# Denominators in four quarters of TensorE's columns, and eight weight operations ahead of the FFN's loop

## The chip, the cores and the metric

The kernel runs on one core of a Trainium2 chip. The time is the device time of one execution in microseconds; the comparison is between medians of several runs.

## The reference

Three stages run one after the other. `B, H, S, D` are 4, 8, 1152, 64; neighbouring queries are averaged in pairs, which leaves 576 queries per head and 2304 tokens of width 512.

```python
q_pool = q.reshape(B, H, S // 2, 2, D).mean(axis=3)
scores = matmul(q_pool, k.transpose(0, 1, 3, 2)) / sqrt(D)
attn = exp(scores - max(scores, -1))
x = matmul(attn / (sum(attn, -1) + 1e-9), v)     # then [2304, 512]
h = x @ w_in                                     # 512 -> 2048
x = (h / (1 + exp(-1.702 * h))) @ w_out          # 2048 -> 512
do_compute = x @ w_skip > 0
logits = x @ w_gate                              # 8 experts
e = argmax(logits); gate = softmax(logits)[e]
out = x; out[do_compute] += gate * (relu(x @ w1[e]) @ w2[e])
```

The weights `w_in` and `w_out` arrive as 64-bit floats.

## The kernel before, in words

Most products on TensorE are of split numbers: an operand is a high part in a reduced fp32 format plus a low part with what is left, and a product is the sum of three.

**Attention** (`attention`, L127) works on 16 pairs of heads; a pair's two heads lie in partitions 0 to 63 and 64 to 127. The loop at the end of the function counts steps, 14 (`NU`) per pair. A step runs one score unit (`score_unit`, L263: products on TensorE, then one exponential on ScalarE into `E`), one unit of row maxima for a pair 19 steps ahead (`max_unit`, L216: products, then a maximum on VectorE), at some steps a group of value products (`av_group`, L300), and sums of `E` on GpSimd (`sum_unit`, L276), whose result is `ds`. At step 10 of pair p stands `den(p - 1)` (L320), which sums `ds` over the 128 partitions by a product with ones: four fp32 products of 288 columns, for each head and half of its queries, into the tile `dn`; ScalarE copies `dn` to `dr`; and one row per head goes to `DEN` in DRAM, by SP's queue (by ScalarE's queue for the last pair). Right behind it in the same step runs `max_rows_put` (L241) for the next pair: a transpose of the row maxima on TensorE (tile `mt`), a high and a low part on VectorE (`mh`, `ml`), and eight DMAs that lay them out in two rows of `M2` (printed as `M` in the profile). The first score unit of the next pair subtracts the maxima by a product of `M2` with ones as the last of its accumulations. Each queue works in the order in which the code issues.

`recip` (L404) reads a batch's denominators back, takes reciprocals on VectorE, and writes them to `RD`.

**The FFN** (`ffn`, L491) takes the tokens in six chunks (`CH`, L34) of 768, 384, 256, 256, 256 and 384; a chunk of 768 is worked in two pieces of 384, the one of 384 in one. For each chunk it goes over 16 blocks (`fb`) of 128 hidden units. A step of the main loop (from L757) is one block and one piece: `layer1` (L591) makes `h` by 12 products on TensorE, a sigmoid on ScalarE, `g = h * sigmoid` on VectorE (L605), the high part `gh` on ScalarE (L606), and the low part `gl` on VectorE (L609). `layer2` follows two steps later (`LAG`) with nine products into `acc`. `h` has two buffers, so the products of step s+2 wait for `g` of step s.

In chunk 0 (32 steps) the weights are converted from 64-bit floats as they are first used. The weights of a block come as two units, `w_in` and `w_out`; a unit takes seven operations on VectorE (L453 to L459) and three on ScalarE (L461 to L463): `wload` (L423) loads it, `wsplit` (L432) gives the operations, and the generator `blocks` (L528) puts them in order. `fill(k)` (L565) gives out the next k of them; `layer1` calls it twice, for 3 and 3 operations in the first piece of a block, 3 and 4 in the second. A unit's first ScalarE operation, the absolute value (L461), is given out when its turn begins, with the load of the unit two ahead; the other two wait in a list that `act` (L571) empties right behind `gh`. Two blocks (`EARLY`) are converted in attention already.

For chunk 1, `xload` (L466) loads X and the reciprocals `RD`, each row of `RD` spread over 64 partitions, into `xraw`, which has one buffer; `xnorm` (L474) multiplies them on VectorE, and `xsplit` (L585) makes the high and low part. The four such loads and products are set down in an agenda, which runs what is due at the end of a step.

**The experts** (`experts`, L874) follow when the last chunk is routed.

Of the kernel before, what the change touches and what calls it, by code (L numbers as in the profile page):

```python
# [9 lines left out]
F32 = mybir.dt.float32  # L10
# [5 lines left out]
AF = mybir.ActivationFunctionType  # L16
# [3 lines left out]
P = 128  # L20

B, H, S, D = 4, 8, 1152, 64
Q = S // 2
HQ = Q // 2
# [15 lines left out]
def pieces(n):  # L40
    k = -(-n // 384)
    return [(i * (n // k), n // k) for i in range(k)]
# [29 lines left out]
class Kernel:  # L72
# [54 lines left out]
    def attention(self, ctx):  # L127
        nc = self.nc
        V, G = nc.vector, nc.gpsimd
        dma = self.dma  # L130
        sm = self.pool(ctx, "a_sm", 2)
# [3 lines left out]
        const = self.pool(ctx, "a_const")  # L135
# [7 lines left out]
        HALF = [slice(64 * u, 64 * u + 64) for u in range(2)]  # L143
        M2 = [const.tile([P, Q], F32R, name=f"M2_{i}") for i in range(2)]
        BD = [const.tile([P, P], F32R, name=f"BD{i}") for i in range(2)]
        ONE = const.tile([P, P], F32R, name="ONE")
        one = const.tile([P, 64], F32, name="one")
        warm = const.tile([P, 2], F32, name="warm")
        V.memset(warm, 0.0)
        nc.scalar.activation(warm[:, 1:2], warm[:, 0:1], AF.Copy)  # L150
# [12 lines left out]
        ag = Agenda()  # L163
# [155 lines left out]

        def den(p):  # L320
            ds = st[p]["ds"]
            dr = sm.tile([P, Q], F32, name="dr", tag="dr", bufs=1)
            ps = slot.tile([P, 2, 512], F32, name="dn", tag="sl")
            for c in range(2):
                for u in range(2):
                    nc.tensor.matmul(ps[HALF[u], c, :HQ], one, ds[:, u, c * HQ:c * HQ + HQ], start=True, stop=True)
            nc.scalar.activation(dr.rearrange("p (a b) -> p a b", a=2), ps[:, :, :HQ], AF.Copy)
            b, hp = divmod(p, H // 2)
            eng = nc.scalar if p == N - 1 else nc.sync
            for u in range(2):  # L330
                eng.dma_start(self.DEN[hp * 2 + u:hp * 2 + u + 1, b * Q:b * Q + Q], dr[64 * u:64 * u + 1])

        LEAD = 19

# [7 lines left out]
        start = {1: [(k_low, 0)], 2: [(q_low, 0)], 4: [(loads, 2)], 5: [(q_add, 1)], 7: [(q_high, 1)], 8: [(k_high, 1, 0)], 9: [(k_high, 1, 1)],  # L342
                 10: [(k_high, 1, 2)], 11: [(v_load, 0)], 13: [(q_add, 2)]}
# [28 lines left out]
        for g in range(-LEAD, NU * N + 20):  # L372
            p, i = divmod(g, NU)
# [117 lines left out]
    def ffn(self, ctx):  # L491
        nc = self.nc
# [6 lines left out]
        sm = self.pool(ctx, "m_sm", reuse_waits="tile")  # L499
        const = self.pool(ctx, "m_const", reuse_waits="tile")  # L500
        hp = self.pool(ctx, "m_h", 2, space=PSUM, reuse_waits="tile")
# [12 lines left out]
        def constants():  # L514
            nc.gpsimd.memset(ONE, 1.0)
            nc.gpsimd.memset(U, 1.0)
            nc.gpsimd.affine_select(out=U, in_=U, compare_op=ALU.is_ge, fill=0.0, base=-1, pattern=[[1, P]], channel_multiplier=-1)
            nc.gpsimd.iota(idi, pattern=[[P, NT]], base=0, channel_multiplier=1)
            for t, step, base in ((w8, -1, 8), (b8, NTOK, 0)):
                nc.gpsimd.iota(i8, pattern=[[step, 8]], base=base, channel_multiplier=0)  # L520
                for i in range(3):
                    nc.gpsimd.tensor_copy(t[:, i], i8)
            V.memset(mac[0], 0.0)

        fq = []
        ag = Agenda()
# [38 lines left out]
        def fill(k):  # L565
            for _ in range(k):
                f = fq.pop(0) if fq else next(splits, None)
                if f:
                    f()

        def act():  # L571
            while after:
                after.pop(0)()
# [17 lines left out]
        def layer1(c, fb, pc, fa, fb_):  # L591
            n = pieces(CH[c])[pc][1]
            h = hp.tile([P, 512], F32, name="h", tag="h")[:, :n]
            ah, al = self.W[fb, "wih"], self.W[fb, "wil"]
            k = 0
            for d in range(ND):
                xh, xl = self.xtile(c, d, pc)
                for a, x in ((ah, xh), (ah, xl), (al, xh)):
                    nc.tensor.matmul(h, a[:, d * P:d * P + P], x, start=(k == 0), stop=(k == 3 * ND - 1))  # L599
                    k += 1  # L600
            g = gp.tile([P, 384], F32, name="g", tag="g")[:, :n]
            gh = g3.tile([P, 384], F32R, name="gh", tag="gh")[:, :n]
            gl = g3.tile([P, 384], F32R, name="gl", tag="gl")[:, :n]
            nc.scalar.activation(g, h, AF.Sigmoid, scale=1.702)  # L604
            V.tensor_tensor(g, h, g, op=ALU.mult)  # L605
            nc.scalar.activation(gh, g, AF.Copy)  # L606
            act()
            fill(fa)
            V.tensor_tensor(gl, g, gh, op=ALU.subtract)  # L609
            fill(fb_)  # L610
            G[c, fb, pc] = (gh, gl)
# [139 lines left out]
                fq.append(fin)  # L751

        constants()
        steps = [(c, fb, pc) for c in range(len(CH)) for fb in range(NF) for pc in range(len(pieces(CH[c])))]
        first = {(c, fb): g for g, (c, fb, pc) in reversed(list(enumerate(steps)))}
        LAG = 2
        for g in range(len(steps) + LAG):  # L757
            ag.now = g
            if g < len(steps):
                c, fb, pc = steps[g]  # L760
                fa, fb_ = (2, 3) if CH[c] >= 384 else (1, 2)
                if g == 2:
                    self.recip(sm, B - 1, ag, 3)
                if c == 0:
                    fa, fb_ = 3, 3 + pc
                layer1(c, fb, pc, fa, fb_)
                if fb == 0 and pc == 0 and c + 1 < len(CH):
                    for j in range(ND):
                        for q in range(len(pieces(CH[c + 1]))):
                            g0 = first[0, 12] + 2 * j - 1 if c == 0 else first[c, 4] + 2 * j  # L770
                            ag.at(g0, xload, c + 1, j, q)
                            ag.at(g0 + 1, xnorm, c + 1, j, q)
                            ag.at(first[c, NF - 1] if c == 0 else g0 + 4, xsplit, c + 1, j, q)
            if g >= LAG:
                c2, f2, p2 = steps[g - LAG]
                layer2(c2, f2, p2)
                if f2 == NF - 1:
                    if c2 == 0 and p2 == 0:
                        while splits.gi_frame:
                            fill(1)  # L780
                            act()
                        rctx.close()
                        late["o"] = self.pool(ctx, "m_o", 2)
                        late["wg"] = late["o"].tile([P, 9, DM], F32, name="wg", tag="wg", bufs=1)
                        dma(late["wg"][:, 0:8], self.wgT.partition_broadcast(P))
                        dma(late["wg"][:, 8], self.w_skip.partition_broadcast(P))
                        for d in range(ND):
                            dma(wgd[:, d, 0:8], self.wgT[:, d * P:d * P + P].rearrange("e p -> p e"))
                            dma(wgd[:, d, 8:9], self.w_skip[d * P:d * P + P].rearrange("(p a) -> p a", a=1))
                    o, n = pieces(CH[c2])[p2]  # L790
                    grp = tuple((C0[c2] + o) // P + i for i in range(n // P))
                    if c2 < len(CH) - 1:
                        todo.extend((grp, i) for i in range(len(grp)))
            if g < len(steps) + LAG - 1:
                rstep()
                ag.run(g)
            if not (self.first or todo or fq or live[0]) and self.listed == NT - CH[-1] // P:

                self.first = late["o"].tile([P, 9, DM], F32, name="first", tag="wg", bufs=1)
                for m in range(4):  # L800
                    self.first_expert_load(m)
                for m in range(8):
                    ag.at(max(g + 2 + m // 2, first[len(CH) - 1, m] + LAG + 1), self.first_expert_split, m)

                ps = hp.tile([P, 8], F32, name="cn", tag="h")
                nc.tensor.matmul(ps, ONE, mac[self.listed], start=True, stop=True)
                V.tensor_scalar(self.early, ps[:, 0:1], P - 0.5, float(P), op0=ALU.is_gt, op1=ALU.mult)
                dma(self.ids_e, self.LIST[0:P])
                V.memset(self.x_e, 0.0)
                nc.gpsimd.indirect_dma_start(  # L810
                    out=self.x_e, out_offset=None, in_=self.X2[0:C0[-1]],
                    in_offset=bass.IndirectOffsetOnAxis(ap=self.ids_e[:, 0:1].bitcast(U32), axis=0),
                    bounds_check=C0[-1] - 1, oob_is_err=False,
                )
# [270 lines left out]
```

## Time and profile before

| what | us |
|---|---|
| median of 3 runs | 1052.24 |
| the runs | 1047.6 to 1054.67 |
| the profiled execution, its time | 1049.92 |
| its span, first to last instruction | 1048.1 |
| TensorE busy in it | 996.8 |
| VectorE busy in it | 768.9 |
| ScalarE busy in it | 501.9 |
| GpSimd busy in it | 454.2 |

All rows of the trace are from the one profiled execution; its times count from the first instruction. Attention ends near 442.7 us, chunk 0 of the FFN takes from there to about 585 us. In the profile PE is TensorE's products and PEld its weight loads, DVE is VectorE, ACT ScalarE, POOL GpSimd, SP the queue of DMAs. "x2" at the end of a row of a timeline tells how many like instructions are merged in it; what stands in brackets is how long the engine was idle before, and what ended that. The end of a product is modelled, so products are read by their starts.

### The profile page before, as it was taken

Reading aid. Unit: us, or ns where it says so; the run is one execution under the profiler, and the core shown is the slowest. Engines: PE = TensorE matmul, PEld = TensorE weight load, DVE = VectorE, ACT = ScalarE, POOL = GpSimd, SP = SyncE. Lnnn points to the kernel's source line nnn. Section 1 sums busy time; section 2 is a strip of 40 time slices with the busy share of each in tenths; the row PEclk is TensorE's granted clock in tenths of the full one; section 3 lists DMA queues with packets and bytes.
Section 4 is the critical chain, followed back from the end, with each engine's and each line's share of the span. In section 5 each row is a group of like instructions: output and inputs, shape, how many; then the busy total and the mean of one; then the engine's idle time right before and its main releaser. Section 6 shows DMA issues by size and latency. Waiting matters only on the chain. (4 is left out here: it accounts for less than half of the span.)

```text
span 1048.1 us, 18986 instructions
## 1 busy us (share of the span) xinstructions
PE 996.8 (95%) x7002; PEld 787.3 (75%) x7002; DVE 768.9 (73%) x1643; ACT 501.9 (48%) x928; POOL 454.2 (43%) x306
## 2 busy tenths in 40 slices
PE   6999999999999999999997999999999997998994
PEld 4766667666766676698886888888889885876773
DVE  7767777778877778799977689787575564656824
ACT  2555555555555554655644422332333261555723
POOL 3798999999999998500000001101111003223212
PEclk9999999999999999999999999999999998998998
DMA  4232232223333322333342520212211234738501
GB/s 166 67 101 81 81 101 82 81 81 97 97 96 96 97 72 71 99 102 122 123 132 81 173 71 16 71 33 60 71 48 44 81 115 145 266 105 285 164 21 51
DMA packets 64321, 103.34 MB, mean 99 GB/s; under 512 B 18630, under 2 KB 34630, under 8 KB 64072
## 3 DMA queue, kind: packets, MB, share of 16 engines
q1 hardware_dynamic: 60068, 96.34, 28.6%
q0 software_dynamic: 3904, 5.15, 1.6%
q8 instruction: 67, 1.10, 0.4%
q14 instruction: 54, 0.44, 0.1%
q10 hardware_dynamic: 228, 0.30, 0.1%
HBM read 90.04 MB, written 17.35 MB: 102 GB/s over the span
## 5 line engine op out<-in xcount | busy, mean ns | idle before, releaser
L233 DVE TENSOR_REDUCE mx<-xs 128x1 f32<-128x384 f32 x432 | 212.7, 550 | 75.5 <-PE xs L230 70.1
L274 ACT ACTIVATE E<-ss 128x640 f32<-128x640 f32 (+1 forms) x224 | 174.0, 787 | 149.0 <-PE ss L273 120.7
L290 POOL TENSOR_TENSOR acc<-acc,E 128x640 f32<-128x640 f32 (+1 forms) x94 | 179.4, 1909 | 16.4 <-ACT E L274 12.3
L310 PE MATMUL av<-E,v 128*64 128x256 f32 (+1 forms) x1152 | 157.1, 413 | 0.0
L599 PE MATMUL h<-xh,wih 128*128 128x384 f32 (+1 forms) x448 | 141.3, 315 | 9.9 <-ACT wih L463 7.7
L599 PE MATMUL h<-xh,wil 128*128 128x384 f32 (+1 forms) x448 | 140.0, 312 | 0.6 <-DVE wil L459 0.5
L599 PE MATMUL h<-xl,wih 128*128 128x384 f32 (+1 forms) x448 | 139.9, 312 | 0.1
L476 POOL TENSOR_TENSOR xa<-xraw 128x256 f32<-128x256 f32 (+1 forms) x16 | 15.5, 970 | 261.3 <-DMA xraw<-RD 256.1
L310 PEld LDWEIGHTS av<-E,v 128*64 128x64 f32 x1152 | 75.6, 136 | 56.0 <-issue 15.0
L626 PE MATMUL acc<-woh,gl 128*128 128x512 f32 x288 | 114.8, 399 | 0.0
L624 PE MATMUL acc<-woh,gh 128*128 128x512 f32 x288 | 114.8, 399 | 0.0
L625 PE MATMUL acc<-wol,gh 128*128 128x512 f32 x288 | 114.5, 398 | 0.0
L230 PE MATMUL xs<-kh,qh 64*128 64x384 f32 x384 | 101.9, 388 | 7.9 <-ACT kh L210 7.2
L273 PE MATMUL ss<-qh,kh 64*128 64x320 f32 (+1 forms) x576 | 107.3, 339 | 2.0 <-ACT E L274 2.0
L604 ACT ACTIVATE g<-h 128x384 f32<-128x384 f32 (+1 forms) x112 | 49.4, 441 | 116.1 <-PE h L599 116.0
L606 ACT ACTIVATE gh<-g 128x384 fp32r<-128x384 f32 (+1 forms) x112 | 53.8, 480 | 104.6 <-DVE g L605 104.6
L599 PEld LDWEIGHTS h<-xh,wih 128*128 128x128 f32 x448 | 84.2, 188 | 18.5 <-ACT wih L463 11.0
L643 DVE CUSTOM_DVE_ANT_0 junk<-xs,wg 128x512 bf16<-128x512 f32 x135 | 95.5, 707 | 2.0
L605 DVE TENSOR_TENSOR g<-h,g 128x384 f32<-128x384 f32 (+1 forms) x112 | 55.7, 497 | 55.9 <-ACT g L604 54.5
L273 PE MATMUL ss<-M,ONE 64*128 64x320 f32 (+1 forms) x576 | 94.2, 294 | 0.7 <-DMA M<-ml 0.6
L273 PE MATMUL ss<-qh,kl 64*128 64x320 f32 (+1 forms) x576 | 92.2, 293 | 0.0
L273 PE MATMUL ss<-ql,kh 64*128 64x320 f32 (+1 forms) x576 | 92.1, 293 | 0.0
(195 smaller groups left out, 2069.6 us busy)
## 6 DMA issues: line engine op xcount, KB each, us to landing
stage<-w SPq DMA_DIRECT2D x40, 512.0 KB
qd<-qT SPq DMA_DIRECT2D x16, 576.0 KB
v<-v SPq DMA_DIRECT2D x16, 576.0 KB
kr<-kT SPq DMA_DIRECT2D x15, 576.0 KB
wr<-w_in SPq DMA_DIRECT2D x16, 512.0 KB
wr<-w_out SPq DMA_DIRECT2D x16, 512.0 KB
X<-xs SPq DMA_DIRECT2D x18, 256.0 KB
out<-xs SPq DMA_DIRECT2D x18, 256.0 KB
```

Source lines behind the costliest of these rows:

```text
L230: nc.tensor.matmul(ps[:, :384], q, k[:, part * 384:part * 384 + 384], start=True, stop=True)
L233: V.reduce_max(o, ps[:, :384], axis=AX.X)
L273: nc.tensor.matmul(ps[:, u, j * w:j * w + w], k[HALF[u]], q[HALF[u], qs], start=(n == 0), stop=(n == 3))
L274: nc.scalar.activation(place(p, i), ps[:, :, :len(kbs) * w], AF.Exp, scale=0.5 / D ** 0.5)
L290: G.tensor_tensor(d["a"], d["a"], place(p, i), op=ALU.add)
L310: nc.tensor.matmul(d["av"][HALF[u], :w], d["v"][:, u, kb], e[:, u, n * w:n * w + w], start=(kb == 0), stop=(kb == KB - 1))
L599: nc.tensor.matmul(h, a[:, d * P:d * P + P], x, start=(k == 0), stop=(k == 3 * ND - 1))
L605: V.tensor_tensor(g, h, g, op=ALU.mult)
L624: nc.tensor.matmul(acc[t], gh[:, ts], bh, start=(fb == 0), stop=False)
L625: nc.tensor.matmul(acc[t], gh[:, ts], bl, start=False, stop=False)
L626: nc.tensor.matmul(acc[t], gl[:, ts], bh, start=False, stop=(fb == NF - 1))
L643: V.tensor_tensor_reduce(out=junk, in0=R[grp[i]], in1=late["wg"][:, e], op0=ALU.mult, op1=ALU.add, scale=1.0, scalar=0.0, accum_out=R[grp] ...
```

## The change

There are two parts. In `den` the tile of ones gets 32 columns instead of 64, and the four products write four quarters of the partitions of one bank; the copy then has 288 columns instead of 576, and four rows of 288 go to `DEN` instead of two of 576. In `ffn`, `fill(8)` stands ahead of the main loop, so the first eight operations of the conversion stand ahead of step 0's; and the loads for chunk 1 are due two steps sooner (steps 21, 23, 25, 27 instead of 23 to 29), each product one step sooner and two steps behind its load instead of one.

```diff
-        one = const.tile([P, 64], F32, name="one")
+        one = const.tile([P, 32], F32, name="one")
...
         def den(p):
             ds = st[p]["ds"]
-            dr = sm.tile([P, Q], F32, name="dr", tag="dr", bufs=1)
+            dr = sm.tile([P, HQ], F32, name="dr", tag="dr", bufs=1)
             ps = slot.tile([P, 2, 512], F32, name="dn", tag="sl")
-            for c in range(2):
-                for u in range(2):
-                    nc.tensor.matmul(ps[HALF[u], c, :HQ], one, ds[:, u, c * HQ:c * HQ + HQ], start=True, stop=True)
-            nc.scalar.activation(dr.rearrange("p (a b) -> p a b", a=2), ps[:, :, :HQ], AF.Copy)
+            quarter = [(slice(64 * u + 32 * c, 64 * u + 32 * c + 32), u, c) for u in range(2) for c in range(2)]
+            for to, u, c in quarter:
+                nc.tensor.matmul(ps[to, 0, :HQ], one, ds[:, u, c * HQ:c * HQ + HQ], start=True, stop=True)
+            nc.scalar.activation(dr, ps[:, 0, :HQ], AF.Copy)
             b, hp = divmod(p, H // 2)
             eng = nc.scalar if p == N - 1 else nc.sync
-            for u in range(2):
-                eng.dma_start(self.DEN[hp * 2 + u:hp * 2 + u + 1, b * Q:b * Q + Q], dr[64 * u:64 * u + 1])
+            for to, u, c in quarter:
+                eng.dma_start(self.DEN[hp * 2 + u:hp * 2 + u + 1, b * Q + c * HQ:b * Q + c * HQ + HQ], dr[to.start:to.start + 1])
...
         constants()
+        fill(8)
         steps = [(c, fb, pc) for c in range(len(CH)) for fb in range(NF) for pc in range(len(pieces(CH[c])))]
...
-                            g0 = first[0, 12] + 2 * j - 1 if c == 0 else first[c, 4] + 2 * j
+                            g0 = first[0, 12] + 2 * j - 3 if c == 0 else first[c, 4] + 2 * j
                             ag.at(g0, xload, c + 1, j, q)
-                            ag.at(g0 + 1, xnorm, c + 1, j, q)
+                            ag.at(g0 + 2 if c == 0 else g0 + 1, xnorm, c + 1, j, q)
```

## Rows read from the trace of the kernel before

**Rows 1.** The page's first part: busy time of each engine, share, instructions.

```profile
PE 996.8 (95%) x7002; PEld 787.3 (75%) x7002; DVE 768.9 (73%) x1643; ACT 501.9 (48%) x928; POOL 454.2 (43%) x306
```

**Rows 2.** Busy time by stretch: its length, PE, PEld, DVE, ACT, POOL, clock, DMA, GB/s.

```profile
92.00:118.00 26.00, 26.00 (x256) 18.16 (x254) 20.18 (x35) 14.49 (x23) 23.81 (x14) 1.00 0.28 82
...
450.00:460.00 10.00, 10.00 (x51) 8.94 (x50) 10.00 (x24) 6.50 (x13) 0.00 (x0) 1.00 0.43 134
...
550.00:560.00 10.00, 7.04 (x28) 6.38 (x29) 8.11 (x17) 4.75 (x9) 0.00 (x0) 0.83 0.29 96
```

**Rows 3.** TensorE's timeline around one pair's denominators: start, length, line, tiles, count.

```profile
94.92 1.14 PE L326 MATMUL dn<-ds,one 128*64 128x288 f32 x8
...
95.41 0.66 PE L326 MATMUL dn<-ds,one 128*64 128x288 f32 x4
...
95.65 0.41 PE L326 MATMUL dn<-ds,one 128*64 128x288 f32 x2
95.99 0.28 PE L243 MATMUL mt<-ident,m 128*9 128x128 f32 x1
96.20 0.39 PE L273 MATMUL ss<-qh,kh 64*128 64x256 f32 x2
```

**Rows 4.** Groups on ScalarE in attention, by shape: busy us, mean ns, idle before.

```profile
L327 ACT ACTIVATE dr<-dn 128x576 f32<-128x576 f32 x15 | 9.8, 654 | 8.0 <-PE dn L326 8.0
...
L314 ACT ACTIVATE ev<-av 128x320 f32<-128x320 f32 x15 | 6.6, 437 | 13.6 <-PE av L310 13.6
```

**Rows 5.** The timeline of SP's queue behind the same denominators.

```profile
96.79 0.53 SPq L331 DMA_DIRECT2D DEN<-dr  x2
97.41 2.47 SPq L252 DMA_DIRECT2D M<-mh  x4
100.01 2.40 SPq L252 DMA_DIRECT2D M<-ml  x4
```

**Rows 6.** The timeline of weight loads at the next pair's first score unit.

```profile
102.72 0.20 PEld L273 LDWEIGHTS ss<-ql,kh 64*128 64x128 f32 x2
102.87 0.29 PEld L273 LDWEIGHTS ss<-M,ONE 64*128 64x128 f32 x2
```

**Rows 7.** TensorE's timeline: first products of steps 0, 2, 26, 28, 32, 33.

```profile
442.67 0.44 PE L599 MATMUL h<-xh,wih 128*128 128x384 f32 x1
...
446.93 0.34 PE L599 MATMUL h<-xh,wih 128*128 128x384 f32 x1
...
552.96 0.45 PE L599 MATMUL h<-xh,wih 128*128 128x384 f32 x1 [3.72 <-ACT wih L463]
...
566.05 0.44 PE L599 MATMUL h<-xh,wih 128*128 128x384 f32 x1 [2.90 <-ACT wih L463]
...
584.99 0.34 PE L599 MATMUL h<-xh,wih 128*128 128x384 f32 x1
...
589.18 0.34 PE L599 MATMUL h<-xh,wih 128*128 128x384 f32 x1
```

**Rows 8.** VectorE's timeline: the start of the FFN, and the first two products for chunk 1.

```profile
441.93 0.06 DVE L523 MEMSET mac<- 128x4 uint32 x1
445.57 0.56 DVE L605 TENSOR_TENSOR g<-h,g 128x384 f32<-128x384 f32 x1 [3.58 <-ACT g L604]
...
550.28 0.56 DVE L476 TENSOR_TENSOR xa<-xraw 128x384 f32<-128x384 f32 x1 [2.34 <-DMA xraw<-RD]
...
563.38 0.56 DVE L476 TENSOR_TENSOR xa<-xraw 128x384 f32<-128x384 f32 x1 [2.82 <-DMA xraw<-RD]
```

**Rows 9.** ScalarE's timeline at the start of the FFN.

```profile
442.79 0.65 ACT L327 ACTIVATE dr<-dn 128x576 f32<-128x576 f32 x1 [0.99 <-PE dn L326]
443.47 0.55 ACTq L331 DMA_DIRECT2D DEN<-dr  x2
...
446.60 1.21 ACT L461 ACTIVATE t<-wr 128x512 f32<-128x512 f32 x2
```

**Rows 10.** The timeline of SP's queue: the first two loads of `RD`.

```profile
543.10 0.53 SPq L83 DMA_DIRECT2D xraw<-RD  x1
...
555.23 0.52 SPq L83 DMA_DIRECT2D xraw<-RD  x1
```

## The prediction

> **What bounds the kernel now.** I read the engines' busy times first, then busy time by stretch, then the timelines of single engines around the two places that the diff touches. Over the whole span TensorE is busy 996.8 of 1048.1 us [rows 1], so a saving counts if TensorE gets to its next work sooner. The stretches say where that is open. In attention, 92 to 118 us, TensorE is busy 26.00 of 26.00 us [rows 2]: attention costs what TensorE's queue costs, unless something else makes it wait. In the FFN's first chunk it is different. A step is 4.19 us when nothing waits (584.99 to 589.18), the first two, without second-layer products, together 4.26 us (442.67 to 446.93) [rows 7]. Step 32, the first of chunk 1, would so start at 442.67 + 4.26 + 30 x 4.19 = 572.6 us. It starts at 584.99 [rows 7]: 12.4 us are stalls. From 550 to 560 us TensorE is busy 7.04 of 10 us and its mean granted clock is 0.83 of 2.4 GHz, a mean between the levels 2.4 and 1.2, behind a wait of 3.72 us for a converted `wih` [rows 2, 7]. From 450 to 460 VectorE is the full one, 10.00 of 10 us for 24 instructions, 0.42 us each [rows 2].
>
> Why the weights come late: a pair of steps gives VectorE 6 + 7 = 13 weight operations, and a block needs 14. Two blocks are ready at the start, so the conversions slide one operation per block from just early to just late. The last step of the slide is made worse by two waits of VectorE for `xraw` (2.34 and 2.82 us, ended by the broadcast of `RD`) [rows 8]: behind them stand `g`, the rest of the weight operations, and TensorE's waits of 3.72 and 2.90 us [rows 7].
>
> **Edit 1, the denominators on TensorE.** Now a pair's denominators are 8 passes (four products of two passes each), two side by side: four waves, 0.24 us apart (95.41 to 95.65), the first at 94.92 [rows 3]. After the last wave `mt` starts 0.34 us later, 0.10 more than a wave; from `mt` to the scores it is 0.21 us, for 128 columns, where a wave of 288 takes 0.24, so 0.11 for the product and again 0.10 for the change of tile shape [rows 3]. Four side by side make two waves: 2 x 0.24 = 0.48 us less. Between the value products (64 columns) and the denominators (now 32) a change of shape appears, 0.10 us. TensorE saves 0.38 us per pair. No row shows four abreast: the ends are no gain (four waves, minus 0.10) and 0.48 us (the change after them falls away); I take two waves, since two abreast start in one row.
>
> **Edit 1, the copy and the DMAs.** ScalarE's copy of 576 columns takes 0.65 us; the nearest row to 288 is 320 columns, 0.44 us [rows 4], so about 0.40: 0.25 saved. But the two DMAs to `DEN` become four on SP's queue, and behind them in that queue stand the eight that build the next pair's row maxima `M`. Two cost 96.79 to 97.41, 0.31 us each with what lies between; eight for `M` follow at 0.6 us each until 102.41 [rows 5]. TensorE's first score unit of the next pair needs `M`: its two weight loads lie at 102.87 and take 0.29 us together, where the pair before took 0.20 [rows 6]. The second was held 0.1 us by the semaphore, without delaying a product: `M` lands just as TensorE arrives, slack at most some 0.05 us. So this chain, not TensorE's queue, decides what edit 1 is worth. Last wave of the denominators: earlier by 2 x 0.24 - 0.10 = 0.38. Copy: 0.25 earlier. DMAs: 2 x 0.31 = 0.62 later. Sum: 0.01 us earlier. TensorE gains 0.38 us on the denominators and waits about 0.3 of it for `M`. With the slack I take 0.06 us per pair, times 14 pairs that have both: 0.8 us. If the queue were no limit: 14 x 0.38 = 5.3 us.
>
> The Trainium skill bears on the four abreast. "TensorE: Matmul & The Clock Gate", section "Part 3: Packing small matmuls — row/col tiling", says that products in different column groups run at once, and gives 2.38 times the rate for three. No run here shows that yet. By that efficiency, an estimate from the page, four would take some 0.6 us instead of 0.48, and the sum would lose 14 x 0.12 = 1.7 us.
>
> The last pair's copy and DMAs are on ScalarE: 0.25 less, two more issues of 0.27 us (0.55 for two) [rows 9]; nothing at TensorE's end of it, since its later products wait for VectorE's last sums as before.
>
> **Edit 2a, eight weight operations first.** VectorE is free from 441.99 to 445.57 [rows 8]. The eight are in order a first one, then seven; the second needs ScalarE's absolute value. That comes behind the copy and four issues: 442.79 + 0.40 + 4 x 0.27 = 444.3, and 0.6 for itself (1.21 for two) [rows 9]: 444.9. Seven operations at 0.42 end at 447.85, and only then comes `g` of step 0, 0.56 us: 448.4 instead of 446.13. Step 2 needs that buffer of `h` and started at 446.93 [rows 7]: TensorE stalls 1.5 to 1.7 us, I take 1.6. Step 2's second-layer products need `gl` only after another 2.5 us, by when three fills and `gl` fit. From there VectorE spends about 3.9 us per step (6.5 fills and two `g` operations at 0.42 plus) against TensorE's 4.19, so nothing more is lost; the weights stand eight operations earlier, a bit over half a block, more than the slide of one per block eats up to the last block. `wih` then is converted one whole step before its use in blocks 10 to 15, and these waits go.
>
> **Edit 2b, the next chunk's operands.** The loads of X and RD come two steps earlier, each product one step earlier and two steps (8.4 us) behind its load. RD was issued at 543.10 and 555.23, VectorE went on at 550.28 and 563.38: 7.2 and 8.15 us [rows 8, 10]. One step could not cover that, two do, nearly: with the load's issue and the product itself the cycle is 8.2 to 9.2 us. VectorE may come up to 0.8 us late per load. But its lateness has cover now: `g` of step s is needed only at step s+2, and the weights are a step ahead. I allow 0.3 us. On SP's queue these loads pass two or three weight loads, each held until VectorE frees its buffer; the first may so wait for one `g` and one weight operation more, about 1 us.
>
> Sum: of 12.4 us stalls 1.6 + 0.3 remain, 10.5 gained, and 0.8 in attention: 11.3 us. All later stages follow chunk 0 and shift with it. The profiled execution took 1049.92 us, so 1038.6 beside it; it lies 2.3 us under the median of the three runs, 1052.24, from which I forecast 1040.9 us.
>
> **Rivals.** (A) `M` has more slack than I read, and edit 1 gives its full 5.3 to 6.7 us on TensorE. For: the stretch where TensorE has no idle time. Against: the held weight load. With 5.8 between these: 1052.24 - 10.5 - 5.8 = 1035.9.
>
> (B) The operands still set the pace: the four RD loads each take 9.2 us against 8.4, VectorE slips 0.8 us each time, 3.3 us in all, and the first load's 1 us adds to it, so TensorE gets 4.3 us of stalls back. For: both RD rows were taken beside 512 KB weight loads, and earlier loads have more of these for company. Against: the cover just named. Gain 10.5 - 4.3 + 0.8 = 7.0: 1045.2.
>
> A sentence of the Trainium skill speaks against B: "DMA: Bandwidth & Descriptors", section "Rules for kernel authors", says that an outermost dimension of few copies confines a DMA to as many engines, and RD's load has two head rows outermost. By that rule its 7.2 us are its own and not the company's, all four loads keep within 8.4, and B falls away; the trace's 7.2 against 8.15 leaves this open.
>
> (C) Four 32-column products don't run side by side: four waves plus a change of shape. Then `M` comes 0.10 - 0.25 + 0.62 - 0.05 = 0.42 us later per pair, 5.9 us in all: gain 4.6, 1047.6.
>
> (D) Slower: a `DEN` issue of 288 columns costs as much as one of the `M` issues, 0.6 us, not 0.31 [rows 5]. The place is SP's queue between the copy and `M`: 4 x 0.65 - 0.62 = 1.98 later, less 0.63 and the slack 0.05: 1.3 us x 14 = 18 us, minus 10.5: 1060. It turns the sign from about 0.51 us per issue on. Against: shorter rows are hardly dearer to issue.
>
> **How the numbers follow.** Forecast 0.49 (own range 1038.5 to 1043), A 0.15, B 0.21, C 0.10, D 0.05. The range reaches from A less 2 us (0.48 instead of 0.38 per pair, and the spread of the runs) to C plus 1 us: 1034 to 1048.5; D lies outside. A measurement of this kernel can tell about 1% (10.5 us). The forecast passes that by 0.8 us, so about 0.36 of its 0.49 and all of A are faster: 0.51. The rest of it, B and C are within 1%: 0.44. D: 0.05.
>
> **What would show it.** Right: eight `dn` passes in two starts 0.24 us apart; `M` loads starting within 0.1 us of where they did relative to the pair; a wait of `ss` for the DMA of `ml` of about 0.3 us per pair; the pairs' period as it is now, to 0.1 us. `g` of step 0 near 448.4 minus attention's shift, one stall of 1.6 us at step 2, no wait of TensorE for `wih` above 0.5 us, no granted clock under 0.95 between steps 20 and 32, step 32 about 131.5 us after step 0 instead of 142.3. Wrong: a pair period down by 0.3 us (A), waits for `xraw` that still reach TensorE (B), `dn` in four starts (C), `DEN` issues near 0.6 us (D).

## The result, and the profile after

The changed kernel takes 1038.69 us, the median of 6 runs (1036.73 to 1041.24); the kernel before, beside it, 1053.14 us (6 runs, 1047.6 to 1054.67). The ratio is 0.9872 with a 95% interval of 0.9843 to 0.99. The forecast was 1040.9. By the medians 14.5 us are gained, where the forecast had 11.3. The profiled execution took 1036.8 us with a span of 1035.1 us, 13.0 us less than the span before; these 13.0 us are what the rows can explain.

Where the 13.0 us come from, by starts on TensorE (a pair is marked by its first denominator product, a step by its first first-layer product):

| stretch | before | after | change | foreseen |
|---|---|---|---|---|
| start of the kernel to pair 0 | 68.47 | 68.51 | +0.04 | 0 |
| pair 0 to pair 13, 13 periods | 339.56 | 338.95 | -0.61 | -0.8 for 14 |
| pair 13 to pair 15 | 33.02 | 30.88 | -2.14 | 0 |
| pair 15 to step 0 | 1.62 | 2.08 | +0.46 | 0 |
| step 0 to step 32 | 142.32 | 131.98 | -10.34 | -10.5 |
| step 32 to the end | 463.11 | 462.70 | -0.41 | 0 |

Attention first. TensorE's timeline at the pair of [rows 3], in two windows: all eight passes, and those that still ran at 95.21; columns are start, length, line and tiles.

```profile
94.75 0.69 PE L326 MATMUL dn<-ds,one 128*32 128x288 f32 x8
95.37 0.28 PE L243 MATMUL mt<-ident,m 128*9 128x128 f32 x1
95.58 0.39 PE L273 MATMUL ss<-qh,kh 64*128 64x256 f32 x2
...
95.02 0.43 PE L326 MATMUL dn<-ds,one 128*32 128x288 f32 x4
```

Four passes start together at 94.75 and four at 95.02: two waves, 0.27 us apart, so the four quarters do run side by side. From the first pass to `mt` it is 0.62 us where [rows 3] have 1.07. What the saving meets is on ScalarE and SP: the group of the copy (count, shortest, median and longest in ns) and SP's queue, against [rows 4, 5].

```profile
L327 ACT ACTIVATE dr<-dn x16: 411/412/413, 69.3 to 440.5; 128x288 f32<-128x288 f32 x16
```

```profile
95.95 1.13 SPq L331 DMA_DIRECT2D DEN<-dr  x4
97.17 2.46 SPq L252 DMA_DIRECT2D M<-mh  x4
100.16 2.45 SPq L252 DMA_DIRECT2D M<-ml  x4
```

`M` begins 2.42 us after the first denominator pass; before it was 2.49. TensorE arrives earlier by more than that, and waits. Here are its line at the product that needs `M`, and its busy time in the stretch of [rows 2].

```profile
103.11 0.41 PE L273 MATMUL ss<-M,ONE 64*128 64x320 f32 x1 [0.40 <-DMA M<-ml]
```

```profile
92.00:118.00 26.00, 25.60 (x252) 17.45 (x250) 19.46 (x35) 14.12 (x23) 23.47 (x14) 1.00 0.28 78
```

The 0.40 us in brackets are the 0.40 us that the stretch is short of 26.00. The lists name such a wait in few pairs, but the starts show it in each. Compare the two heads' products with `M` in the next pair's first score unit: in the changed kernel the second starts 0.18 to 0.83 us behind the first in each of the 14 pairs, 0.34 us at the median; before it was 0.02 us or less in nine of them. Now the FFN: the same stretches as in [rows 2], then the lines that answer to [rows 7 to 9] on TensorE, VectorE and ScalarE at its start.

```profile
450.00:460.00 10.00, 10.00 (x52) 8.99 (x51) 10.00 (x23) 6.62 (x14) 0.00 (x0) 1.00 0.46 137
550.00:560.00 10.00, 10.00 (x51) 8.89 (x50) 9.04 (x21) 5.57 (x12) 0.00 (x0) 1.00 0.40 123
```

```profile
440.42 0.45 PE L599 MATMUL h<-xh,wih 128*128 128x384 f32 x1
...
446.57 0.45 PE L599 MATMUL h<-xh,wih 128*128 128x384 f32 x1 [1.71 <-DVE g L605]
...
572.40 0.34 PE L599 MATMUL h<-xh,wih 128*128 128x384 f32 x1
```

```profile
442.94 0.43 DVE L454 TENSOR_SCALAR t<-t 128x512 f32<-128x512 f32 x1 [2.84 <-ACT t L461]
...
445.96 0.55 DVE L605 TENSOR_TENSOR g<-h,g 128x384 f32<-128x384 f32 x1
```

```profile
440.55 0.41 ACT L327 ACTIVATE dr<-dn 128x288 f32<-128x288 f32 x1 [0.99 <-PE dn L326]
440.99 1.16 ACTq L331 DMA_DIRECT2D DEN<-dr  x4
442.25 1.24 ACT L461 ACTIVATE t<-wr 128x512 f32<-128x512 f32 x2 [1.29 <-DMA DEN<-dr]
```

Read downwards in time: the four issues hold ScalarE till 442.15, its absolute value lets VectorE go at 442.94, seven weight operations later `g` starts at 445.96, and TensorE takes up step 2 at 446.57 instead of 444.69 (two steps of 2.08 to 2.19 after step 0). That is a stall of 1.88 us. No other wait of TensorE is listed up to step 32, which starts at 572.40, 131.98 us after step 0. From 550 to 560 us TensorE is busy all the time at full clock, where it had 7.04 us and 0.83. VectorE still waits for `RD`, 3.3 us in two waits, and none of it reaches TensorE.

### The profile page after: what moved, and what is told of

It is laid out like the page before. It is cut to its first block, busy times and chain, and to the rows that moved or that the text cites. A ratio compares the mean times of both kernels' runs of the same rounds, so it can differ in the third digit from the quotient of the medians.

```text
span 1035.1 us, 19024 instructions
## 1 busy us (share of the span) xinstructions
PE 990.2 (96%) x7002; PEld 779.6 (75%) x7002; DVE 762.7 (74%) x1643; ACT 497.5 (48%) x928; POOL 459.8 (44%) x306
## 5 line engine op out<-in xcount | busy, mean ns | idle before, releaser
L273 PE MATMUL ss<-M,ONE 64*128 64x320 f32 (+1 forms) x576 | 98.1, 295 | 2.1 <-DMA M<-ml 1.9
```

What stands on the lines that cost most here:

```text
L273: nc.tensor.matmul(ps[:, u, j * w:j * w + w], k[HALF[u]], q[HALF[u], qs], start=(n == 0), stop=(n == 3))
```

## The experiments

All runs are shown beside runs of the kernel before on the same chip. A diff of a part undone shows it against the changed kernel.

**The two edits by themselves.** The loop of the FFN put back, so that the denominators alone are changed:

```diff
-        fill(8)
-                            g0 = first[0, 12] + 2 * j - 3 if c == 0 else first[c, 4] + 2 * j
+                            g0 = first[0, 12] + 2 * j - 1 if c == 0 else first[c, 4] + 2 * j
...
-                            ag.at(g0 + 2 if c == 0 else g0 + 1, xnorm, c + 1, j, q)
+                            ag.at(g0 + 1, xnorm, c + 1, j, q)
```

> The kernel before with the first part of the change alone. Theory (the row maxima's DMAs decide): TensorE saves 0.4 us on each pair's denominators and waits nearly all of it for the next pair's maxima, so the first 13 pair periods shrink by 0.05 us each, 0.6 us in all; with the last two pairs, behind which no maxima stand, step 0 of the FFN starts 2 to 2.5 us sooner, and step 32 follows it 142.3 us later as before: 2.3 us faster than before. Rival (TensorE's queue decides): 13 x 0.38 + 2 = 7 us faster. Rival (the last pairs' gain isn't the denominators'): under 1 us.

Measured: 1052.36 us against 1054.95, ratio 0.9974 (0.9945 to 1.0004). The 13 periods take 339.71 us, pair 13 to 15 30.90, and step 0 starts at 441.46; the unchanged attention of the next three runs has 340.2, 33.0 to 34.5 and 443.7 to 445.2. So the first edit brings some 0.5 us in the periods and 2 us in the last two pairs; the time alone, whose interval reaches past 1, can't show it. Step 32 comes 143.52 us after step 0, where 142.3 was foreseen, although the FFN is as before; the run with four DMAs below, with the same FFN, has 144.24. So this stretch differs by up to 1.9 us between executions of the same loop.

The reverse, `den` put back as before (its tile of 64 ones, four products in halves, copy of 576, two DMAs):

> The kernel before with the second part alone (eight operations ahead, loads sooner). Theory: the two parts don't touch each other; attention is as before (step 0 at 442.7 us), step 32 comes 131.5 to 132.5 us behind step 0 instead of 142.3: 10 to 10.5 us faster. Since the last pair has two DMA issues on ScalarE and a longer copy, the stall at step 2 is 1.4 to 1.9 us. Rival (the parts need each other): below 8 us.

Measured: 1043.39 us, ratio 0.9898 (0.9861 to 0.9935). Step 32 starts 131.64 us after step 0, with one stall of 1.52 us at step 2. All of the gain in the FFN comes with the second edit.

**The second edit's halves**, both with `den` as before. First the eight operations alone, with the loads put back:

```diff
-                            g0 = first[0, 12] + 2 * j - 3 if c == 0 else first[c, 4] + 2 * j
+                            g0 = first[0, 12] + 2 * j - 1 if c == 0 else first[c, 4] + 2 * j
...
-                            ag.at(g0 + 2 if c == 0 else g0 + 1, xnorm, c + 1, j, q)
+                            ag.at(g0 + 1, xnorm, c + 1, j, q)
```

> The kernel before with the eight operations ahead, the loads for chunk 1 where they were. Theory (the lead of the conversion is the cover, the loads' waits reach TensorE only for want of it): TensorE's waits for converted weights in blocks 10 to 14 go, VectorE still waits 2 to 3 us for each of the first loads; the last load is late for step 32 by 2 to 3 us. Step 32 comes 133 to 136 us behind step 0, 6.5 to 9.5 us faster. Rival (the loads are the cause): 139 us or more, 3 us or less.

Measured: 1052.48 us, ratio 0.9979 (0.9953 to 1.0004). This missed. Step 32 does start at +134.76 us, but step 35 at +153.53, where the kernel before has 154.88: most of what is won by step 32 is lost inside it, where it needs chunk 1's operands. TensorE's waits from 436 to 600 us (total, times, longest), then its line within step 32 and VectorE's ahead of it:

```profile
PE h L599 <- ACT xh L485: 2.9, 1, 2.9
PE h L599 <- DVE g L605: 2.6, 2, 1.4
PE h L599 <- ACT wih L463: 1.5, 1, 1.5
```

```profile
583.04 0.69 PE L599 MATMUL h<-xh,wih 128*128 128x384 f32 x1 [2.89 <-ACT xh L485]
```

```profile
581.87 0.56 DVE L476 TENSOR_TENSOR xa<-xraw 128x384 f32<-128x384 f32 x1 [4.33 <-DMA xraw<-RD]
```

Step 32 so takes 9.85 us instead of 4.19. The wait is 2.89 us of that; behind it TensorE ran at a granted clock of 0.50 from 583 to 589 us, the lower level, with its first-layer products 0.32 us apart instead of 0.17.

With the product one step behind its load, VectorE stands for `RD` three times, 9.9 us in all, and the loads start 9.4 to 11.5 us apart, each held by the product before. Four such turns end after step 32 has begun. So weights that stand ahead don't cover the loads.

Now the loads alone, without the eight operations:

```diff
-        fill(8)
```

> The kernel before with the loads for chunk 1 sooner, no operation ahead. Theory: the slide of one operation per block stays, with its waits of 0.3 to 0.6 us in blocks 10 to 15, and what VectorE still waits for the loads reaches TensorE in full; no stall at step 2. Step 32 comes 135 to 140 us behind step 0, 3 to 7 us faster. Rival (the loads are the cause): 133 us or less, 9 us or more, as much as both edits together.

Measured: 1046.13 us, ratio 0.9923 (0.9901 to 0.9944). Step 35 comes 148.19 us after step 0, 6.7 less than before; no wait for `xraw` is left, and the slide still is, as many small waits:

```profile
PE h L599 <- ACT wih L463: 2.6, 4, 0.8
PE h L599 <- DVE wil L459: 0.5, 1, 0.5
```

By the start of step 35, behind the last of these waits, the eight operations alone bring 1.35 us, the loads alone 6.7, both 10.2 (144.65, in the run of the second edit alone). Each of these hangs on the 154.88 of one execution before; the same loop stands at 156.08 and 156.80 in the runs with the denominators alone and with four DMAs. By the medians of the times the three gains are 2.5 (not clear of noise), 8.8 and 11.6 us, so the halves about add up; that one is worth more with the other is not shown.

**What SP's issues cost.** Everything as before, but each pair's denominators stored by four DMAs in place of two:

```diff
-            for u in range(2):
-                eng.dma_start(self.DEN[hp * 2 + u:hp * 2 + u + 1, b * Q:b * Q + Q], dr[64 * u:64 * u + 1])
+            for u in range(2):
+                for c in range(2):
+                    eng.dma_start(self.DEN[hp * 2 + u:hp * 2 + u + 1, b * Q + c * HQ:b * Q + c * HQ + HQ], dr[64 * u:64 * u + 1, c * HQ:c * HQ + HQ])
```

> The kernel before, its products and copy untouched, but each head's row of denominators goes out in two DMAs of 288, so four issues stand on SP's queue instead of two. Theory (the maxima behind them have no slack): the maxima start 0.6 us later in each pair and TensorE waits 0.5 to 0.6 us more; the 13 pair periods from the first to the fourteenth denominators grow from 339.6 to 340.2 us together to 346 to 348. Rival (TensorE's queue decides, DMA issues are hidden): they stay within 1 us.

Measured: 1058.17 us in one run; 13 periods in 345.74 us, 0.3 under the foreseen span and 6.2 more than before, 0.47 per pair. SP's queue and TensorE's waits from 40 to 432 us:

```profile
96.72 1.13 SPq L332 DMA_DIRECT2D DEN<-dr  x4
97.94 2.46 SPq L252 DMA_DIRECT2D M<-mh  x4
```

```profile
PE ss L273 <- DMA M<-ml: 4.2, 11, 0.7
```

The first issue of `M` now comes 1.22 us after that of `DEN`, where [rows 5] have 0.62. Two issues cost 0.60 us on SP, and all but 0.13 of it is on the path of the pairs. The next two runs take the issues out of the way of the new products. First, `DEN` issued after `M`:

```diff
-            for to, u, c in quarter:
-                eng.dma_start(self.DEN[hp * 2 + u:hp * 2 + u + 1, b * Q + c * HQ:b * Q + c * HQ + HQ], dr[to.start:to.start + 1])
+            def put():
+                for to, u, c in quarter:
+                    eng.dma_start(self.DEN[hp * 2 + u:hp * 2 + u + 1, b * Q + c * HQ:b * Q + c * HQ + HQ], dr[to.start:to.start + 1])
+            put() if p == N - 1 else ag.at(ag.now + 1, put)
```

> The changed kernel with the four DMAs of the denominators given out one step later, so behind the maxima's eight on SP's queue. Theory: the maxima start about 1.2 us sooner, TensorE no longer waits for them, and keeps the 0.35 us that the quarters save in each pair: the 13 periods shrink from 339.0 us to 334 to 336, the whole kernel is 3 to 5 us faster than the changed kernel, 1.6 to 1.9% faster than before. Rival (another wait stands as close behind, VectorE's maxima or ScalarE's exponentials): less than 1 us off the 13 periods.

Measured: 1033.6 us, ratio 0.9802 (0.9756 to 0.9848). 13 periods take 334.53 us, a period 25.66; TensorE waits for no `M` at all. SP's queue:

```profile
96.21 2.48 SPq L252 DMA_DIRECT2D M<-mh  x4
98.79 2.43 SPq L252 DMA_DIRECT2D M<-ml  x4
101.75 1.11 SPq L333 DMA_DIRECT2D DEN<-dr  x4
```

One thing here was not foreseen: the stall at step 2 is 0.27 us and not 1.88, though `g` starts 5.49 us after step 0 as it did (5.54). The stretches at the start of the FFN show why (columns as in [rows 2]):

```profile
434.00:437.00 3.00, 1.42 (x9) 0.45 (x10) 2.48 (x6) 1.98 (x5) 0.42 (x1) 1.00 0.04 16
437.00:440.00 3.00, 3.00 (x10) 3.00 (x11) 0.69 (x2) 1.62 (x3) 0.00 (x0) 0.52 0.21 84
```

TensorE was busy 1.42 of 3 us, waiting for VectorE's last sums, and then ran step 0 at a granted clock of 0.52, close to the lower level of 1.2 GHz: its products are 0.32 us apart, not 0.17. Step 0 so took 1.57 us longer, and 1.57 + 0.27 is nearly the stall again. TensorE stood twice here, 0.58 us ahead of the last pair's first product at 434.52 and, two passes later, 1.06 us; in the next run, where the clock stayed at 1.00, it stood once:

```profile
436.23 0.69 PE L326 MATMUL dn<-ds,one 128*32 128x288 f32 x6 [1.06 <-DVE mac L527]
```

```profile
437.06 0.69 PE L326 MATMUL dn<-ds,one 128*32 128x288 f32 x6 [1.00 <-DVE mac L522]
```

No run tried whether the second stop is what lowered the clock.

Second, one DMA per pair, for which `DEN` gets another shape and `recip` reads it straight:

```diff
-            self.DEN = dram.tile([H, NTOK], F32, name="DEN")
+            self.DEN = dram.tile([B, 2 * H, HQ], F32, name="DEN")
-            for to, u, c in quarter:
-                eng.dma_start(self.DEN[hp * 2 + u:hp * 2 + u + 1, b * Q + c * HQ:b * Q + c * HQ + HQ], dr[to.start:to.start + 1])
+            eng.dma_start(self.DEN[b, hp * 4:hp * 4 + 4], dr[0:P:32])
-        self.dma(t, self.DEN[:, b * Q:b * Q + Q].rearrange("h (t c) -> h t c", c=36))
+        self.dma(t, self.DEN[b].rearrange("h (t c) -> h t c", c=36))
```

> The changed kernel with the denominators laid out in DRAM so that a pair's four rows go out in one DMA. Theory: one issue instead of four frees SP's queue 0.9 us sooner, more than the 0.35 us that TensorE could use, so the 13 periods come to the same 334 to 336 us as with the rows behind the maxima. In the last pair ScalarE has one issue instead of four ahead of its first absolute value, so VectorE's wait for that falls by 0.8 us and the stall at step 2 from 1.88 to about 1.0 us: 4 to 6 us faster than the changed kernel in all. Rival (the stall at step 2 is the eight operations alone): it stays at 1.9.

Measured: 1034.14 us, ratio 0.9811 (0.9776 to 0.9845). The 13 periods take 335.32 us, 25.65 or 25.67 where nothing special happens, and the stall at step 2 is 1.36 us, since ScalarE issues one DMA for the last pair and not four. SP's queue:

```profile
96.84 0.53 SPq L330 DMA_DIRECT2D DEN<-dr  x1
97.46 2.43 SPq L252 DMA_DIRECT2D M<-mh  x4
```

Two ways of freeing the queue meet at the same period, and in both TensorE is busy 26.00 of 26.00 us from 92 to 118 us. With `DEN` behind `M`, the two heads' products with `M` start within 0.02 us of each other in all 14 pairs. 25.66 us is TensorE's own, so the new products save 0.33 us per pair (from 25.99; over all 13 periods 0.33 with one DMA and 0.39 with `DEN` behind `M`), and the four DMAs kept 0.29 of it back (25.95).

**How far ahead.** Four operations in place of eight in the changed kernel:

```diff
-        fill(8)
+        fill(4)
```

> The changed kernel with four operations ahead of the loop instead of eight. Theory (each operation that stands behind the absolute value and ahead of the first g is paid for in the stall at step 2, and each less takes a block's worth of lead from the end): the stall at step 2 falls from 1.88 to 0.2 to 0.4 us, blocks 14 and 15 get waits of 0.3 to 0.8 us back; step 32 comes 131 to 132.3 us behind step 0, with eight it is 132.0. Rival (the lead matters little): 130.5 us or less.

Measured: 1041.86 us in one run. The stall at step 2 is 0.13 us, and steps 28 and 30 start 1.19 and 0.88 us late, more than foreseen; step 32 comes at +132.41, 0.4 later than with eight and just past the foreseen span. The waits are exchanged one for the other.

**The best of these together.** One DMA per pair, and the last pair's on SP too, so that ScalarE's absolute value need not wait:

```diff
-            eng = nc.scalar if p == N - 1 else nc.sync
+            eng = nc.sync
```

> The version with one DMA to DEN per pair, and the last pair's DMA moved from ScalarE's queue to SP's. ScalarE's first absolute value then starts right behind the copy, some 0.7 us sooner than in the version with one DMA (38.99 - 38.20 of that trace's 400s), and so VectorE's seven operations and g of step 0. My theory: TensorE's stall at step 2 falls from 1.36 to about 0.65 us, the pairs' 13 periods stay at 334.5 to 336 us, nothing else moves; time against before as the version with one DMA or 0.7 us less. Rival: SP's queue is held by weight loads there, DEN lands late, and ScalarE or VectorE wait for a load of the first chunk's RD at some later point: the stall goes but a new wait appears between steps 2 and 20.

Measured: 1034.88 us against 1052.62, ratio 0.9811 (0.9765 to 0.9857). ScalarE goes from the copy straight to the absolute value:

```profile
437.63 0.41 ACT L327 ACTIVATE dr<-dn 128x288 f32<-128x288 f32 x1 [0.98 <-PE dn L326]
437.94 1.21 ACT L460 ACTIVATE t<-wr 128x512 f32<-128x512 f32 x2
```

The stall is 0.47 us, 0.89 less than 1.36, and step 32 starts at +130.73, 0.84 sooner; no new wait appears. The time alone can't show so little. Then six ahead in this kernel:

```diff
-        fill(8)
+        fill(6)
```

> As the run with the last pair's DMA on SP's queue, with six weight operations given out ahead where that has eight. Eight ahead: the stall at step 2 alone (1.88 us with four DMAs). Four ahead, with four DMAs: 0.13 us there, and 1.19 and 0.88 us in steps 28 and 30. My theory: six lie between, no stall at step 2 over 0.2 us, and at steps 28 to 31 waits of together 0 to 1 us. Rival: the slide is decided in whole operations, and with two short the waits at steps 28 and 30 are those of four ahead, 2 us; then eight is no worse than six.

Measured: 1032.01 us (1029.34 to 1032.93), ratio 0.9791 (0.975 to 0.9832). From step 0 to step 32 it is 129.87 us: the 4.26 + 30 x 4.19 = 129.96 us of steps without any stall. TensorE's waits from 436 to 575 us are down to the one for the last sums of attention:

```profile
PE dn L326 <- DVE mac L522: 1.0, 1, 1.0
```

This version, 0.9791 of the kernel before where the change makes 0.9872, is faster than both; the two intervals don't overlap. Six can't be told from eight by the time (0.9811, 0.9765 to 0.9857); by the start of step 32 it is 0.86 us sooner.

## Why the prediction was right, and where it wasn't

**Edit 1: the chain to `M`.** `M` was to start 0.01 us earlier. Measured: the issues cost 0.60, the copy saves 0.24, and from the last value product to the first issue of `M` it is 2.78 us, 2.76 before, so 0.02 later. Per pair it gave 0.61 / 13 = 0.05 us, against 0.06. The runs with one DMA, and with `DEN` behind `M`, show that SP's queue is what kept the rest back: freed of it, the period falls by 0.33 to 0.39. That is the mechanism of rival A, which needed slack that wasn't there. TensorE's saving itself was put at 0.38; the waves are 0.27 us apart and not 0.24, and the change of shape costs 0.10 as taken (0.36 us from the last value product to the first denominator, 0.26 before). The wait of about 0.3 us per pair is there: the lists show only 5, 1.9 us in all, but the second head's product with `M` starts late in every pair, by 0.34 us at the median.

The Trainium skill's rate for three products side by side ("TensorE: Matmul & The Clock Gate", "Part 3: Packing small matmuls — row/col tiling") had given an estimate of some 0.6 us for the two waves. By TensorE's starts two waves are 2 x 0.27 = 0.54 us, between the prediction's 0.48 and that 0.6. With SP's queue in the way the difference couldn't show in the time.

**Edit 2: the FFN's start.** `g` was expected to end 448.4 - 442.67 = 5.73 us after step 0; it ended 6.09 after (it starts 5.54 after and takes 0.55). Of these 0.36 us, 0.29 are there when VectorE goes on behind the absolute value, 2.52 us after step 0 where the prediction has 444.9 - 442.67 = 2.23. The stall at step 2, taken at 1.6 us, was 1.88 with four issues on ScalarE and 1.52 where `den` was left alone. Its cause was as written: the issue of the last pair's DMAs, then ScalarE's absolute value, then seven operations. The runs with one DMA (1.36), with that on SP (0.47) and with six operations (none) take it down piece by piece.

**Edit 2: the rest of chunk 0.** 10.34 us came of 10.5, with no wait for `wih`. Step 32 came 131.98 us after step 0; the prediction's own terms give 4.26 + 30 x 4.19 + 1.9 = 131.86, not the 131.5 among its signs. That the term fits to 0.2 us is luck in part: the loop as before differs by 1.9 us from one execution to the next. Rival B fell, but not for want of its premise: the four loads of `RD` start 9.3, 8.3 and 9.2 us apart, near B's 9.2, and VectorE still waits for them, 3.3 us in two places. It is the cover that keeps this from TensorE. What the prediction hadn't separated is how the halves share the gain. It saw VectorE's waits for `xraw` ahead of TensorE's waits of 3.72 and 2.90 us, but counted on the weights ahead to take these away. Alone, the weights bring 1.35 us, and the loads 6.7, about the sum of these two waits. My expectation for the weights alone was wrong in the same way: it looked at step 32's start, and the loads of chunk 1 hold that step from inside.

**Rivals C and D** fell by the rows: two starts and not four, and 0.28 us per issue of 288 columns (four in 1.13), not 0.6.

**The step that failed**, by 1.7 us: "nothing at TensorE's end of it", said of the last pair, with pair 14 left out of the "14 pairs that have both". Pair 13 to pair 15 takes 2.14 us less; 0.46 us of it is lost again in a longer wait for the last sums. The seven traces with the quarters have 30.7 to 30.9 us there. Four of the five with the products as before have 33.0, the one with four DMAs among them; the fifth has 34.5, and there TensorE ran behind a wait at a granted clock of 0.84 and 0.74 for 8 us.

The plain part of the 2.14 is pair 14: no maxima stand behind its denominators, so it keeps what the quarters save, and its period goes from 8.01 to 7.66 us, 0.35 less. Pair 13 keeps 0.35 too, less 0.12 more of waiting for `M`.

The larger part, 1.5 us, lies in the last pair's score units: from the third to the sixth it is 4.20 us instead of 5.71. Before, TensorE waits 1.43 us at the fourth for ScalarE's `E` of the second. Ahead of that `E` in ScalarE's order stands `xh`, a conversion for the FFN, which waits for the product `xraw` on VectorE:

```profile
419.26 0.53 ACT L485 ACTIVATE xh<-xraw 128x384 fp32r<-128x384 f32 x1 [1.75 <-DVE xraw L476]
420.21 0.68 ACT L274 ACTIVATE E<-ss 128x640 f32<-128x640 f32 x1
```

```profile
420.95 0.41 PE L273 MATMUL ss<-qh,kh 64*128 64x320 f32 x2 [1.43 <-ACT E L274]
```

After, `xh` waits no more, and the fourth unit starts at once:

```profile
416.47 0.52 ACT L485 ACTIVATE xh<-xraw 128x384 fp32r<-128x384 f32 x1
417.40 0.70 ACT L274 ACTIVATE E<-ss 128x640 f32<-128x640 f32 x1
```

```profile
418.42 0.31 PE L273 MATMUL ss<-qh,kh 64*128 64x320 f32 x2
```

What changed stands earlier, on VectorE and on GpSimd. Before:

```profile
409.42 0.28 DVE L246 TENSOR_SCALAR mh<-mt 9x128 fp32r<-9x128 f32 x1 [2.78 <-PE mt L243]
...
409.94 2.19 DVE L454 TENSOR_SCALAR t<-t 128x512 f32<-128x512 f32 x1
...
417.34 1.89 DVE L476 TENSOR_TENSOR xraw<-xraw 128x384 f32<-128x384 f32 x1
```

```profile
409.44 2.40 POOL L288 TENSOR_TENSOR acc<-E 128x1024 f32<-128x1024 f32 x1
```

And after:

```profile
408.40 0.28 DVE L246 TENSOR_SCALAR mh<-mt 9x128 fp32r<-9x128 f32 x1 [2.43 <-PE mt L243]
...
408.92 0.40 DVE L454 TENSOR_SCALAR t<-t 128x512 f32<-128x512 f32 x1
...
410.19 0.54 DVE L476 TENSOR_TENSOR xraw<-xraw 128x384 f32<-128x384 f32 x1
```

```profile
408.78 4.78 POOL L288 TENSOR_TENSOR acc<-E 128x1024 f32<-128x1024 f32 x1
```

The same operations take 2.19 or 0.40 us on VectorE, and the same sum 2.40 or 4.78 us on GpSimd. Whichever comes behind is slowed, and after the change it is GpSimd, which nobody waits for there. VectorE's work behind `mt` began 0.02 us ahead of that sum before (409.42) and 0.38 ahead of it after (408.40), since `mt` comes 1.02 us sooner and the sum 0.66; that turned the order round. The product for the conversion comes 7.15 us sooner, and the wait behind it goes. That the order decides is read from these rows. All twelve traces agree: the sum takes 4.8 us in the seven with the quarters, and 2.4 us in the five without. But no run changed the order by itself, so the cause of this part is argued and not shown.

The forecast's 11.3 us of gain and the 13.0 of the span differ by this 2.14 - 0.46, by 0.41 in the stages after chunk 0, which vary by more than that between profiled executions, and by -0.39 in the small misses of the other terms.

## What to carry to other kernels

Count a saving along the chain that ends last, with every DMA issue that the edit adds in front of a waiting queue: here a saving of 0.33 us per pair on the busiest engine was worth 0.05 until the issues ahead of `M` were fewer or stood behind it. Work given out ahead brings little while the other operand of the same loop comes late, and how much to give out is a number to try: eight operations had a stall at the start and four at the end; six, tried with one DMA per pair on SP, had neither. Try the halves of an edit apart and follow them beyond the step where the gain shows, since a later wait may take it back.

## What the runs showed of the hardware

VectorE and GpSimd don't run these operations side by side at their own pace: 0.40 against 2.19 us and 2.40 against 4.78 us for one and the same instruction, by which stood first. The Trainium skill has a rule for this in "SBUF — State Buffer", section "Summary: rules for kernel authors": where VectorE is in its two-port mode, or has two inputs in SBUF while GpSimd's operation reads SBUF, the second to issue blocks until the first is done. The trace agrees in that one side alone pays each time. After the change the wait lasts for more than one operation: the sum on GpSimd takes 2.38 us longer, about as long as the five operations of VectorE from 408.92 to 411.33 us.

Four passes of products of 32 columns, 288 wide, start within 0.02 us of each other, and the next four 0.27 us later. A DMA of four rows of 1152 bytes costs SP 0.53 us to issue as one instruction, and 1.13 us as four.
